# A fused attention and mixer kernel on one core: engines in program order, 1 KB load runs, a wide index load, gated weights

## The chip, the cores and the metric

The kernel runs on one core of one Trainium2 chip. The metric is the device time of one execution in microseconds. The kernel before takes 393.94 us (median of three runs, 393.15 to 394.01). "Span" is the length of the one execution that was profiled; it is some 0.3 to 4 us shorter than the median time. Positions such as "at 87.4 us" are counted from the start of the span.

## The reference

Eight batches go through a windowed attention with eight global tokens and then through a token-and-channel mixer. Cut to what matters:

```python
# q, k, v: (8 batches, 8 heads, 576, 64) f32; global_idx: 8 sorted positions, int64
scores = q @ k.T / 8, kept where |i - j| <= 32 or i or j is global
x = softmax(scores) @ v                       # heads side by side: (8, 576, 512)
u = x + (relu(x.T @ w_tok1) @ w_tok2).T       # w_tok1 576x256, w_tok2 256x576
out = u + relu(u @ w_ch1) @ w_ch2             # w_ch1 512x1536, w_ch2 1536x512
```

## The kernel before

Per batch the work falls into a "sparse" and a "dense" part. The sparse part is attention and token mixer: transposes `T` of q and k (tile `pT`), scores `S_` (tile `s`), keys and outputs of the global tokens `GK` and `OG` (tiles `gk`, `og`), P.V (tile `pv`), then the token matmuls `M1` (tile `a1p`) and `M2` (tile `hp`), whose result plus x is u. `M3` transposes u into uT. The dense part is the channel mixer: `M4` (tile `b1p`, 12 pieces) reads uT, `M5` (tile `op`) writes the output. The function `merge` weaves the sparse part of batch b+1 into the dense part of batch b. Batch 0 has no dense part to hide behind: everything before its first `b1p` is the start.

The parts that the argument touches:

```python
# index list: 8 of 16 int32 words per partition, so 1,024 pieces of 4 bytes in all
nc.scalar.dma_start(out=gidx_b, in_=bass.AP(tensor=gt32, offset=0, ap=[[0, P], [2, NG]]))
# [...] q and k of batch 0 head by head in 256-byte runs, then v, on the sync queue

def globals_(b):                       # global keys into q's tile: needed by the first scores
    nc.gpsimd.tensor_copy(out=qTs[b % 2][:, :, :, 0:NG], in_=gT[:, b]...)

def PV(b, tau):
    ps = psv([P, 2, 512], name=f"pv_{b}_{tau}")        # the only buffer of its kind
    # [...] 18 matmuls, then reciprocal and multiply on VectorE

def M3(b, part):                       # u -> uT by DMA, for every batch
    nc.sync.dma_start_transpose(out=s["uT"][:, :, ...], in_=s["u16"][:, tau, :])

# start; the tile scheduler may move instructions
for p in range(NP):
    cast0(p); T(0, p)
    if p == 0: gather_t(0); globals_(0)
    S_(0, p)
for c in range(NT): castv0(c)          # v: f32 -> f16 on GpSimd
GK(0); OG(0)
# load_wc1, load_wc2, load(1), gather(1), five PV, M1, M2, M3 of batch 0 [...]
gather_t(1)
for b in range(B):
    # [...]
    merge(sparse(b + 1) if b + 1 < B else [], dense(b))
```

The softmax here doesn't subtract the row's maximum and nothing guards it: scores larger than these inputs give would overflow.

## Time and profile before

| stage of the kernel before | from, us | to, us | what limits it |
|---|---|---|---|
| to the first scores | 0 | 44.6 | loads, then a copy on GpSimd |
| first scores to first `og` | 44.6 | 58.6 | scores, exponentials, masks |
| `og` to the first `b1p` | 58.6 | 87.35 | P.V, token matmuls, transposing of u |
| two batches, for instance | 166.6 | 244.7 | TensorE, 78.2 us for a pair |
| last dense part and store | 361.0 | 391.9 | TensorE, then the store |

The busy table of the page, kernel before. Its columns are engine, busy us, share of the span, instructions:

```profile
span 391.9 us, 6622 instructions
...
PE 319.8 (82%) x2697; PEld 167.3 (43%) x2697; DVE 185.6 (47%) x400; ACT 137.2 (35%) x269; POOL 114.7 (29%) x156
```

TensorE (PE) is busy for 82% on average. The average hides two very different stages, as the busy table in stretches shows. Its columns: stretch, its length, the busy time of each engine with its instruction count, the granted TensorE clock, the mean DMA share and GB/s:

```profile
0.00:30.00 30.00, 2.14 (x17) 1.65 (x17) 13.83 (x70) 2.80 (x6) 12.49 (x28) 1.00 0.69 113
...
58.60:87.35 28.75, 17.21 (x149) 9.61 (x149) 12.69 (x27) 2.49 (x4) 20.81 (x26) 0.82 1.58 114
...
166.56:244.72 78.16, 76.71 (x675) 39.97 (x673) 42.19 (x80) 32.89 (x65) 25.83 (x32) 1.00 0.88 92
```

In the loop TensorE works 76.7 of 78.2 us. In the first 30 us it works 2.1, and in the 29 us before the loop 17.2. The clock column is an upper bound there: this profile has no clock record before 67.4 us, and the view counts what is missing as 1.00.

The waits of TensorE in the first 90 us, kernel before (who waited for whom; us in total, times, longest):

```profile
PE pT_0_266 L347 <- ACT qn_79 L328: 23.1, 1, 23.1
PE s_0_0_288 L364 <- POOL qT_168 L339: 14.5, 1, 14.5
PE pT_0_266 L347 <- DVE kn_81 L328: 4.8, 1, 4.8
```

The first line is the wait for q to land and be cast. The DMA view of the stretch from 4 to 12 us says why it is so long:

```profile
DMA packets 807, 0.00 MB, mean 0 GB/s; under 512 B 807, under 2 KB 807, under 8 KB 807
## 3 DMA queue, kind: packets, MB, share of 16 engines
q10 hardware_dynamic: 807, 0.00, 4.4%
```

For 8 us nothing moved but the 4-byte pieces of the index list (queue q10). The q and k loads had been issued on another queue and moved nothing: that queue stood for 8.9 us (3.9 to 12.8 us). The pieces went at 101 a us, so about 0.16 us a piece if 16 engines shared them evenly (an estimate from the 101), though the engines were busy with them for only 4.4% of the time. The second wait, 14.5 us, is the first score matmul behind the copy of the global keys, which GpSimd does only after a cast of v.

The waits of TensorE from 90 to 345 us, kernel before, the longest three:

```profile
PE b1p_0_3083 L509 <- DMA uT_3004<-u_5_2972: 1.3, 1, 1.3
PE b1p_0_1117 L509 <- DMA uT_1038<-u_1_1006: 0.8, 1, 0.8
PE b1p_0_2100 L509 <- DMA uT_2021<-u_3_1989: 0.7, 1, 0.7
```

Only these three batch ends of the stretch wait for the transposed u.

### The profile page before, as it was taken

The page shows a single profiled execution, that of the slowest core. Times are in us where ns is not written, and L with a number is a line of the kernel's source. Part 1 is how long each engine was busy: PE and PEld are TensorE (multiplying, and loading weights), DVE is VectorE, ACT ScalarE, POOL GpSimd, SP SyncE. Part 2 cuts the span into 40 slices and gives each one's busy share as a digit, 9 for nine tenths or more (in the row PEclk, how much of TensorE's full clock was granted, in tenths as well). Part 3 has the DMA queues.
Part 4 walks back from the last instruction along what each step waited for, and adds up shares of the span by engine and source line. Part 5 has one row for each costly group of instructions (what it writes and reads, how often), then busy time and mean ns, then how long its engine had stood idle before and what let it go on. Part 6 is the DMA issues. An engine that isn't in the chain of part 4 may idle for free.

```text
span 391.9 us, 6622 instructions
## 1 busy us (share of the span) xinstructions
PE 319.8 (82%) x2697; PEld 167.3 (43%) x2697; DVE 185.6 (47%) x400; ACT 137.2 (35%) x269; POOL 114.7 (29%) x156
## 2 busy tenths in 40 slices
PE   0010255659999999999999999999899999997995
PEld 0010234324454465444544654455446545453552
DVE  5342254344645563566445635664456356644012
ACT  2001250106710861077118610761086107710610
POOL 4520798922820372028203720282000000000000
PEclk9999999688999999999999999999999999999999
DMA  0799999991985398419853984298600041005012
GB/s 14 122 198 206 182 141 94 122 114 8 125 79 147 21 115 75 136 30 129 79 147 22 117 75 135 35 126 81 145 0 2 28 136 28 2 28 149 0 55 80
DMA packets 143071, 34.56 MB, mean 88 GB/s; under 512 B 134336, under 2 KB 138304, under 8 KB 143040
## 3 DMA queue, kind: packets, MB, share of 16 engines
q0 software_dynamic: 102832, 16.42, 56.1%
q1 hardware_dynamic: 33776, 8.26, 11.2%
q10 hardware_dynamic: 6432, 9.44, 7.2%
q8 instruction: 21, 0.34, 0.4%
q14 instruction: 10, 0.08, 0.1%
HBM read 36.11 MB, written 9.44 MB: 116 GB/s over the span
## 4 chain that ended last, share of the span: by engine, by line
PE 59%; ACT 9%; DMA 3%; DVE 1%; SPq 1%; issue 1%; ACTq 0%
ACT e_all L374 2%; ACT e_all L383 2%; ACT e_all L382 1%; ACT e_all L381 1%; SPq L498 1%; DMA out_dram<-osb_0_2979 1%; DMA uT_3972<-u_7_3940 1%; PE op_4_4213 L535 1%; PE op_2_3013 L535 1%; PE op_2_2030 L535 1%; PE op_2_1047 L535 1%; PE op_2_3981 L535 1%; PE op_0_2938 L535 1%; PE op_0_3463 L535 1%; PE op_3_4197 L535 1%
## 5 line engine op out<-in xcount | busy, mean ns | idle before, releaser
L509 PEld LDWEIGHTS <-wc_184 128*128 128x128 f16 x384 | 33.0, 98 | 45.1 <-issue 15.8
L390 DVE TENSOR_TENSOR e_all<-e_all,bandm 128x1040 f16<-128x1040 f16 x64 | 42.4, 704 | 0.5
L123 POOL DMA_DIRECT2D qn_80<-in_q_dram x20 | 17.5, 873 | 60.6 <-PE pT_3_1738 L347 22.8
L439 PEld LDWEIGHTS <-e_all 128*128 128x128 f16 x320 | 25.2, 101 | 2.1 <-issue 1.0
L123 POOL DMA_DIRECT2D qn_79<-in_q_dram x15 | 13.2, 883 | 40.2 <-PE pT_3_1217 L347 20.1
L384 DVE TENSOR_TENSOR eg<-e_all,bandm 128x160 f16<-128x160 f16 x32 | 7.7, 242 | 31.0 <-ACT e_all L383 31.0
L128 POOL DMA_DIRECT2D vsh_84<-in_v_dram x20 | 16.9, 865 | 14.4 <-PE pv_2_916 L444 1.5
L347 PE MATMUL pT_0_266<-ident,qn_79 128*128 128x128 f16 x5 | 0.7, 309 | 23.1 <-ACT qn_79 L328 23.1
L444 PEld LDWEIGHTS <-e_all 128*128 128x128 f16 x256 | 19.0, 101 | 1.3
L347 PEld LDWEIGHTS <-qn_79 128*128 128x128 f16 x80 | 6.1, 106 | 28.4 <-ACT qn_79 L328 23.1
L364 PEld LDWEIGHTS <-kT_170 64*128 64x128 f16 x160 | 6.2, 103 | 27.4 <-issue 13.8
L123 POOL DMA_DIRECT2D kn_82<-in_k_dram x20 | 17.6, 878 | 0.0
L128 POOL DMA_DIRECT2D vsh_83<-in_v_dram x15 | 12.7, 881 | 9.6 <-PE b1lp_0_1385 L522 1.1
L328 ACT CAST qn_79<-n_q 64x128 f16<-64x128 f32 (+1 forms) x8 | 3.4, 456 | 32.8 <-DMA n_q<-in_q_dram 32.8
L481 PEld LDWEIGHTS <-w_183 128*128 128x128 f16 x80 | 8.2, 103 | 12.6 <-issue 4.8
L123 POOL DMA_DIRECT2D kn_81<-in_k_dram x15 | 13.3, 888 | 0.0
L364 PE MATMUL s_0_0_288<-qT_168,kT_170 64*128 64x208 f16 x4 | 0.5, 357 | 14.5 <-POOL qT_168 L339 14.5
L336 POOL CAST vsh_83<-n_v 32x512 f16<-32x512 f32 (+1 forms) x9 | 6.2, 697 | 19.3 <-DMA n_v<-in_v_dram 19.1
L522 PEld LDWEIGHTS <-wc_184 128*128 128x128 f16 x192 | 11.1, 98 | 0.6
L364 PEld LDWEIGHTS <-kT_171 64*128 64x128 f16 x160 | 5.2, 95 | 12.8 <-issue 8.5
L463 PEld LDWEIGHTS <-w_181 128*128 128x128 f16 x64 | 6.3, 101 | 6.4 <-issue 1.9
L539 DVE TENSOR_TENSOR osb_0_4162<-u_7_3940,op_0_4149 128x512 f32<-128x512 f16 x1 | 0.7, 689 | 17.1 <-PE op_0_4149 L535 17.1
(1059 smaller groups left out, 821.1 us busy)
## 6 DMA issues: line engine op xcount, KB each, us to landing
qn_80<-in_q_dram POOLq DMA_DIRECT2D x16, 128.0 KB, 4.6
kn_82<-in_k_dram POOLq DMA_DIRECT2D x16, 128.0 KB, 4.6
wc_184<-in_moe_w_ch_dram POOLq DMA_DIRECT2D x3, 512.0 KB, 10.3
wc_185<-in_moe_w_ch_dram POOLq DMA_DIRECT2D x3, 512.0 KB, 8.0
vsh_84<-in_v_dram POOLq DMA_DIRECT2D x12, 128.0 KB, 3.5
qn_79<-in_q_dram POOLq DMA_DIRECT2D x12, 128.0 KB, 4.2
kn_81<-in_k_dram POOLq DMA_DIRECT2D x12, 128.0 KB, 4.2
n_q<-in_q_dram SPq DMA_DIRECT2D x9, 128.0 KB, 7.6
```

Of the source, the lines that this page charges most:

```text
L123: nc.gpsimd.dma_start(out=dst[b % 2][0:n, t], in_=ten[b, :, P * t : P * t + n, :].rearrange("h p d -> p h d"))
L128: nc.gpsimd.dma_start(out=vsh[b % 2][r0:r1, c, :, 0:D], in_=v[b, :, j0 : j0 + (r1 - r0), :].rearrange("h p d -> p h d"),)
L364: nc.tensor.matmul(ps[:, par, off : off + n], lhsT=kT[r, P * c : P * c + P], rhs=qf[r, lo : lo + n], start=True, stop=True,)
L374: nc.scalar.activation(out=e2[:, :, 1:3, 64:EW], in_=s1[:, :, 0 : 2 * W].rearrange("p h (c x) -> p h c x", c=2), func=AF.Exp, scale=scale)
L383: nc.scalar.activation(out=e2[:, :, 3, 64:EW], in_=s2[:, :, 2 * QS : 2 * QS + W], func=AF.Exp, scale=scale)
L390: nc.vector.tensor_mul(out=eh, in0=eh, in1=bandm)
L439: nc.tensor.matmul(o, lhsT=e_all[:, h, tau, EW - P - sh : EW - sh], rhs=vsh[b % 2][:, tau, h, :], start=False, stop=last and tau == NT - 1,)
L444: nc.tensor.matmul(o, lhsT=e_all[:, h, tau + 1, 0:P], rhs=vsh[b % 2][:, tau + 1, h, :], start=False, stop=last)
L481: nc.tensor.matmul(ps[:, i, :], lhsT=w2[:, ch, P * tau - sh : P * tau - sh + P], rhs=s["a1"][:, ch, :], start=(ch == 0), stop=(ch == 1),)
L509: nc.tensor.matmul(ps, lhsT=wc1[:, cc, P * j : P * j + P], rhs=s["uT"][:, cc, :], start=(cc == 0), stop=(cc == 3))
L522: nc.tensor.matmul(ps[:, i, :], lhsT=wc1[:, cc, P * j : P * j + P], rhs=s["uTl"][:, cc, :], start=(cc == 0), stop=(cc == 3),)
L535: nc.tensor.matmul(ps, lhsT=w, rhs=wc2[:, j, :], start=(j == 0), stop=(j == NJ - 1))
```

## The change

Its intent: start the dense work earlier and spend less time on changes of TensorE's tile shape. All engines now run in program order, and the weave of the loop groups matmuls of one shape. The first two batches of q and k come in runs of four rows (1 KB) and are put in order when they leave PSUM. The index list comes as one 64-byte row per partition. The channel weights are issued only behind casts. Besides, and not in the headline: the global keys are copied on VectorE, P.V has two half-size buffers, batch 1 is loaded like batch 0 on the sync queue, the output stores moved from ScalarE's queue to the sync queue, zeroing moved from VectorE to GpSimd, and batch 0's u is transposed on TensorE.

The core of the diff (cuts marked):

```diff
-    psV = ctx.enter_context(tc.tile_pool(name="psV", bufs=1, ...PSUM))
+    psV = ctx.enter_context(tc.tile_pool(name="psV", bufs=2, ...PSUM))
+    ctx.enter_context(tc.manual_schedule())
-    gidx_b = const.tile([P, NG], I32)
+    gidx_b = const.tile([P, NG, 2], I32)
-    nc.scalar.dma_start(out=gidx_b, in_=bass.AP(... ap=[[0, P], [2, NG]]))
+    nc.scalar.dma_start(out=gidx_b.rearrange("p g w -> p (g w)"), in_=bass.AP(... ap=[[0, P], [1, 2 * NG]]))
+    def load_qk(b, hs):      # 1 KB runs: partition p holds rows 4p .. 4p+3
+        for ten, dst in ((q, lq), (k, lk)):
+            nc.sync.dma_start(out=dst[:, hs].rearrange("p h i d -> p h (i d)"),
+                in_=ten[b, hs, 0 : S - LAST, :].rearrange("h (p i) d -> p h (i d)", i=4))
-    nc.vector.memset(e_all[:, :, :, 0:64], 0.0)     # and the other zeroing
+    nc.gpsimd.memset(e_all[:, :, :, 0:64], 0.0)
     def globals_(b):
-        nc.gpsimd.tensor_copy(
+        nc.vector.tensor_copy(
     # [...] PV: two tiles [P, 512] instead of one [P, 2, 512]
     def M3(b, part):
+        if part < 2 and b == 0:
+            pu = psv([P, 2, 4, P], F16, name=f"pu_{b}_{part}")   # 8 transposes on TensorE, one copy
     def sparse(b):           # (weight, piece); merge places by weight
-        u += [(0.6, lambda p=p: T(b, p)) for p in range(2)]
-        # [...]
-        u += [(3.0, lambda: None)]
+        u = [(8.0 if b == 1 else 0.5, lambda: globals_(b))]
+        u += [t(0), t(1), sa(0), sb(0), t(2), sm(0), ...]        # t(p): weight 1.0
+        # [...]
+        u += [(6.0, lambda: (M2(b, 2), M3(b, 2) if b % 2 else None))]
     # [...] start: castv(0), then load_wc1; after batch 1's casts of q and k, load_wc2; then castv(1)
```

## The prediction

> **What bounds the kernel now.** Three stretches, by the busy table in stretches and TensorE's timeline. (1) The start: the first dense matmul (b1p of batch 0) begins at 87.4 us; TensorE is under 60% busy until 70 us. (2) From 87.4 to 361 us the dense part of batch b is mixed with the attention of batch b+1; TensorE is 97-99% busy, 78.2 us for two batches. (3) The last dense part and store, 31 us.
>
> **The start.** Two things hold the first q and k tiles. The index load (1,024 four-byte packets on its queue, landing 14.4 us after its issue): the DMA packets show about 106 of these a microsecond from 3 to 13 us, and no q or k packet between 4 and 12 us. Then the weights share the engines until 34 us (q and k get 40 KB/us, against 215-245 alone). The first scores wait for the global keys, copied on GpSimd behind the cast of v (the wait of 14.5 us); they start at 44.6 us and take 3.85 us per head pair.
>
> After the change the index is one 64-byte packet per partition, q and k are 1 KB packets, wc1 is issued after the casts of v, wc2 after batch 1's casts, and the global keys are copied on VectorE. First head pair at 6-8 us, all of q and k by 13 us. VectorE in program order is then the limit: per head pair a cast 0.6, four copies about 1.5, three mask products 1.6 us, and once 8 us of masks and gather: done near 34 us. P.V with the first token matmul takes about 10 us, then relu, two adds of 1.2 us and the transposes on TensorE: first dense matmul at about 53 us, a gain near 34 us. All of it is on the critical path.
>
> **Steady state.** A change of tile shape costs 0.09-0.10 us: a matmul before a score starts the next 0.315 us later, against 0.216. [...] The order shows 123 changes against 143: 2 us. Two P.V buffers and ordered ScalarE work may remove 3 us of short waits.
>
> Against that stands the end of each batch. From the end of the first token-output matmuls (hp) to uT ready takes 7.8 us: one add of 1.22, four transposes of 1.24 issued one after the other, 2.4 landing. In the new order TensorE has 5.2 us of work there when b is odd, 6.5 when even, and the next batch's first transposes now stand behind b1p_0. So TensorE should wait about 2.5 us at each odd and 1.3 at each even boundary, against 0.8-1.3 at odd ones alone before: some 9 us lost.
>
> Sum: 394 - 34 - 2 - 3 + 9 = 364 us. Range 354 to 377.
>
> **What would show it right.** First b1p_0 near 53 us (48-59); no gap in q/k packets between 4 and 12 us; the 78 us pair becomes 79-82 us; waits of TensorE at b1p_0 for the DMA of uT, about 2.5 and 1.3 us.
>
> **What would make it wrong.** The start may be set by v, wc1 or the gather instead of VectorE (first dense matmul past 60 us); wc2, issued late, may hold the first M5; or the transposes may be ready sooner than I count, which gives 9 us more gain.
>
> Chances: faster by over 2% 0.95, within 2% 0.04, slower 0.01.

## The result and the profile after

The changed kernel takes 376.04 us (median of four runs, 375.0 to 377.74), against 393.98 us for the kernel before in the same rounds. The ratio is 0.9549, with a 95% interval of 0.9503 to 0.9596. Ratios here and below are the mean time of one kernel's fast runs over that of the other's fast runs of the same rounds, so not quite the ratio of the medians. The experiments ran in different rounds, in which the median of the kernel before itself lay between 393.98 and 395.35 us. So a difference between the medians of two experiments is uncertain by some 1.4 us.

The busy table of the page and the stretches, kernel after:

```profile
span 375.8 us, 6776 instructions
...
PE 319.2 (85%) x2713; PEld 168.2 (45%) x2713; DVE 202.4 (54%) x507; ACT 136.6 (36%) x269; POOL 117.3 (31%) x167
```

```profile
0.00:20.80 20.80, 3.71 (x27) 2.55 (x28) 12.64 (x44) 2.92 (x5) 17.86 (x41) 1.00 0.93 204
...
36.60:58.45 21.85, 14.79 (x138) 8.72 (x139) 13.03 (x33) 1.59 (x3) 15.58 (x19) 0.92 1.02 210
...
144.12:225.63 81.51, 76.99 (x672) 40.34 (x673) 44.48 (x109) 32.71 (x65) 25.14 (x30) 0.98 0.85 89
```

The first scores now begin at 20.8 us, the first `og` at 36.6, the first `b1p` at 58.45. But a pair of batches takes 81.5 us instead of 78.2, with the same TensorE work. Set against the kernel before on the two spans: the start gave 28.9 us, the first mixed batch (dense part of batch 0) cost 4.8, the rest of the loop 7.8; together 16.3 gained, the spans differ by 16.1.

The waits of TensorE in the first 90 us, kernel after:

```profile
PE pT_0_215 L370 <- ACT qn_83 L352: 8.7, 1, 8.7
PE pg_260 L325 <- DVE g_q_168 L324: 3.2, 1, 3.2
PE pcol_238 L283 <- DVE isgb L279: 3.2, 1, 3.2
PE pT_2_314 L370 <- DVE kn_85 L352: 2.5, 1, 2.5
PE pg_260 L325 <- DVE g_k_170 L324: 2.0, 1, 2.0
```

The two long waits are gone; four of these five are now waits for VectorE. The DMA view from 4 to 12 us, kernel after, answers the one of before:

```profile
DMA packets 2769, 2.15 MB, mean 268 GB/s; under 512 B 859, under 2 KB 2734, under 8 KB 2769
...
q1 hardware_dynamic: 2576, 2.07, 90.1%
...
q10 hardware_dynamic: 124, 0.01, 0.8%
```

Where nothing landed before, 2 MB now land, q and k above all. The waits of TensorE from 90 to 345 us, kernel after:

```profile
PE b1p_0_2209 L571 <- DMA uT_2150<-u_3_2136: 2.8, 1, 2.8
PE b1p_0_3240 L571 <- DMA uT_3181<-u_5_3167: 2.7, 1, 2.7
PE b1p_0_1178 L571 <- DMA uT_1111<-u_1_1104: 2.6, 1, 2.6
PE b1p_0_4240 L571 <- DMA uT_4197<-u_7_4183: 2.5, 1, 2.5
PE b1p_0_2760 L571 <- DMA uT_2695<-u_4_2678: 1.4, 1, 1.4
PE b1p_0_3776 L571 <- DMA uT_3726<-u_6_3709: 1.3, 1, 1.3
```

Now every batch end of the loop waits for uT: 2.5 to 2.8 us where the batch is odd, 1.3 to 1.4 where it is even. (The even end of batch 2 is put down to VectorE by the same view, with 1.2 us.) The seven together are 14.5 us, 9.8 more than before. The stretches on either side of the first of these ends, kernel after, show something else:

```profile
97.30:100.70 3.40, 0.36 (x2) 0.29 (x3) 1.55 (x7) 0.00 (x0) 0.00 (x0) 1.00 0.68 132
100.70:104.10 3.40, 3.11 (x15) 1.78 (x15) 0.14 (x1) 0.60 (x1) 0.00 (x0) 0.50 0.30 97
```

TensorE's granted clock is 0.50 for a record of 3.41 us that begins at 100.7 us, right after the wait. It costs about 1.7 us, half of the record's length. There are three such records in the loop after, behind the ends of batches 1, 3 and 5, and none in the loop before once its first `b1p` are over (one record ends at 91.3 us).

### The profile page after: what moved, and what is told of

It is laid out like the page before. It is cut to its first block, busy times and chain, and to the rows that moved or that the text cites. A ratio compares the mean times of both kernels' runs of the same rounds, so it can differ in the third digit from the quotient of the medians.

```text
span 375.8 us, 6776 instructions
## 1 busy us (share of the span) xinstructions
PE 319.2 (85%) x2713; PEld 168.2 (45%) x2713; DVE 202.4 (54%) x507; ACT 136.6 (36%) x269; POOL 117.3 (31%) x167
## 4 chain that ended last, share of the span: by engine, by line
PE 71%; DVE 12%; ACT 6%; DMA 6%; SPq 3%; issue 2%; DVEq 0%; ACTq 0%
SPq L560 3%; DMA lq<-in_q_dram 1%; DVE e_all L434 1%; ACT e_all L415 1%; ACT e_all L424 1%; DMA uT_1111<-u_1_1104 1%; ACT e_all L422 1%; ACT e_all L423 1%; PE op_4_4431 L597 1%; PE op_3_3737 L597 1%; PE op_4_1695 L597 1%; PE op_3_2706 L597 1%; PE op_3_4415 L597 1%; PE op_2_4399 L597 1%; PE op_1_4383 L597 1%
## 5 line engine op out<-in xcount | busy, mean ns | idle before, releaser
L571 PEld LDWEIGHTS <-wc_180 128*128 128x128 f16 x384 | 32.8, 99 | 55.1 <-issue 22.4
L340 POOL DMA_DIRECT2D qn_83<-in_q_dram x15 | 13.5, 898 | 46.1 <-PE pT_3_1297 L370 23.4
L340 POOL DMA_DIRECT2D qn_84<-in_q_dram x15 | 13.2, 879 | 40.8 <-PE pT_3_2873 L370 20.1
L345 POOL DMA_DIRECT2D vsh_87<-in_v_dram x15 | 12.8, 895 | 16.6 <-PE pv_1_1_1516 L489 2.5
L345 POOL DMA_DIRECT2D vsh_88<-in_v_dram x15 | 12.6, 839 | 16.0 <-PE pv_1_1_982 L489 1.5
L340 POOL DMA_DIRECT2D kn_85<-in_k_dram x15 | 13.6, 907 | 0.0
L532 PEld LDWEIGHTS <-w_179 128*128 128x128 f16 x80 | 7.9, 100 | 12.2 <-issue 4.3
L340 POOL DMA_DIRECT2D kn_86<-in_k_dram x15 | 13.3, 888 | 0.0
L370 PEld LDWEIGHTS <-qn_83 128*128 128x128 f16 x80 | 7.1, 119 | 13.6 <-ACT qn_83 L352 9.2
L584 PEld LDWEIGHTS <-wc_180 128*128 128x128 f16 x192 | 10.9, 98 | 0.6
L370 PEld LDWEIGHTS <-kn_85 128*128 128x128 f16 x80 | 6.8, 120 | 4.8 <-DVE kn_85 L352 4.4
L512 PEld LDWEIGHTS <-w_177 128*128 128x128 f16 x64 | 5.6, 99 | 5.0
L370 PEld LDWEIGHTS <-qn_84 128*128 128x128 f16 x80 | 5.7, 98 | 3.5
L597 PEld LDWEIGHTS <-b_7_4239 128*128 128x128 f16 x48 | 4.7, 98 | 5.4
```

The source lines that it names most:

```text
L340: nc.gpsimd.dma_start(out=dst[b % 2][0:n, t], in_=ten[b, :, P * t : P * t + n, :].rearrange("h p d -> p h d"))
L345: nc.gpsimd.dma_start(out=vsh[b % 2][r0:r1, c, :, 0:D], in_=v[b, :, j0 : j0 + (r1 - r0), :].rearrange("h p d -> p h d"),)
L370: nc.tensor.transpose(out=pT[:, ti, P * t : P * t + P], in_=n[b % 2][:, t, 2 * p : 2 * p + 2, :], identity=ident)
L532: nc.tensor.matmul(ps[:, i, :], lhsT=w2[:, ch, P * tau - sh : P * tau - sh + P], rhs=s["a1"][:, ch, :], start=(ch == 0), stop=(ch == 1),)
L571: nc.tensor.matmul(ps, lhsT=wc1[:, cc, P * j : P * j + P], rhs=s["uT"][:, cc, :], start=(cc == 0), stop=(cc == 3))
L584: nc.tensor.matmul(ps[:, i, :], lhsT=wc1[:, cc, P * j : P * j + P], rhs=s["uTl"][:, cc, :], start=(cc == 0), stop=(cc == 3),)
```

## The experiments

There are two questions. What made the start shorter, and what took back a large part of it? For the first, the theory was that the index row and the copy of the global keys do it; the rivals were the 1 KB runs, the gated weights, and the program order. For the second, the theory was that the batch ends are at fault, because the next batch's transposes moved behind the first `b1p`; the rival was that the transposed u is late whatever stands before it.

### One: the next batch's transposes ahead of the first `b1p`

```diff
-        return (1.0, lambda: (T(b, p), TE(b, p)))
+        return (0.0 if b > 1 and p < 2 else 1.0, lambda: (T(b, p), TE(b, p)))
-    u = [(8.0 if b == 1 else 0.5, lambda: globals_(b))]
+    u = [(8.0 if b == 1 else 0.0, lambda: globals_(b))]
```

> The kernel after, with the next batch's first two groups of transposes (and its first two score matmuls) put ahead of b1p_0, as the kernel before had them. Theory 1 (the loop loses at the end of each batch, where TensorE waits for the transposed u): the waits at b1p_0, 3.0 us at odd and 1.5 at even boundaries, fall below 0.5 us, the half-clock record of 3.4 us that follows each odd boundary goes, the odd batches pay about 1.2 us for a relu that is now uncovered; about 363 us. Rival (the loop is slower because VectorE and ScalarE have more work in it): the two batches stay at 81 us and the total at 375-376.

Measured: 365.49 us (363.49 to 366.99), ratio 0.9256 (0.922 to 0.9291). The waits of TensorE from 90 to 345 us in this run, and TensorE in order of time at the end of batch 3:

```profile
PE s L404 <- DVE kT L393: 3.5, 6, 0.7
PE hp L532 <- ACT a L516: 3.5, 3, 1.2
PE b1p L571 <- DMA uT<-u: 1.2, 1, 1.2
```

```profile
174.51 0.44 PE L370 MATMUL pT<-ident,kn 128*128 128x128 f16 x5
175.52 0.35 PE L404 MATMUL s<-qT,kT 64*128 64x208 f16 x4 [0.57 <-DVE kT L393]
175.81 1.04 PE L571 MATMUL b1p<-uT,wc 128*128 128x512 f16 x4
```

The first `b1p` now follows the scores without a wait, a pair of batches takes 77.8 us, and there is no record of half clock in the loop. Two edited lines gave back 10.5 us of the medians (376.04 to 365.49); by the ratios it is 11.5. The theory is confirmed. The view also shows what is left: 0.6 to 0.7 us at six ends before the first scores, whose q and k have just been transposed, and up to 1.2 us at the relu between `a1p` and `hp`. The 1.2 us at `b1p` are the end of batch 7, which has no next batch whose transposes could go ahead.

### Two: the token matmuls earlier instead

```diff
-        u += [(6.0, lambda: (M2(b, 2), M3(b, 2) if b % 2 else None))]
+        u += [(10.0, lambda: (M2(b, 2), M3(b, 2) if b % 2 else None))]
```

> The kernel after, with the last weight of the attention list 10 instead of 6, so that the token matmuls come earlier and more dense matmuls stand between hp and the next b1p_0 (7.8 us at odd, 9.1 at even boundaries). Theory 1: the same as for the transposes put ahead: waits under 0.5 us, no half clock, about 363 us. Rival (VectorE and ScalarE work): 375-376, or slower, since the attention is squeezed into fewer dense matmuls.

Measured: 369.66 us (367.57 to 369.94), ratio 0.9331 (0.9291 to 0.9371). A larger last weight leaves more dense work behind the token matmuls. The 363 us that I expected were missed. It covers the even ends wholly and leaves 1.3 and 1.5 us at the ends of batches 3 and 5. New waits come from the narrower weave: 0.7 us between scores and 0.8 us before `pv`, three times each, and 1.2 us at the relu, four times. So it is the work between u and its reader that matters, and the transposes are the cheaper way to put it there. No record of half clock falls on these shorter waits.

### Three: the zeroing of e_all away from GpSimd

In the start, one cast of VectorE lasts as long as GpSimd's memset beside it. VectorE, kernel after, in order of time:

```profile
17.13 2.33 DVE L324 CAST g_k_170<-g_k_166 128x128 f16<-128x128 f32 x1
```

GpSimd at the same moment, kernel after:

```profile
17.12 2.26 POOL L254 MEMSET e_all<- 128x2560 f16 x1
19.33 0.60 POOL L255 MEMSET e_all<- 128x512 f16 x1
```

The same cast takes 0.21 us in the kernel before. Here it begins just as the memset does and ends with it (2.33 us beside 2.26). Why they would hold each other up, no run here shows. The run below tests whether the memset is what stretches the cast.

```diff
-    nc.gpsimd.memset(e_all[:, :, :, 0:64], 0.0)      # and two more
+    for h in range(H):
+        zero_(e_all[:, h, :, 0:64])                  # nc.scalar.copy from a zero tile, after cast0(1)
```

> The kernel after, with the three memsets of e_all in the start taken from GpSimd to ScalarE, which is idle then. Theory 2 [...]: the cast of g_k takes 0.2 us instead of 2.33, and the first b1p_0 comes 2 to 3 us earlier, total 373-374. Rival (the cast only looks long, and the gathered keys or the DMA were late): b1p_0 stays at 58.4 us.

Measured: 374.01 us (373.38 to 375.57), ratio 0.9466 (0.9426 to 0.9505). VectorE in this run:

```profile
17.11 0.65 DVE L330 CAST g_k<-g_k 128x128 f16<-128x128 f32 x1
```

The first `b1p` begins at 54.65 us instead of 58.45. Only part of these 3.8 us is the zeroing's. The first `og` begins at 34.59 us instead of 36.56, 2.0 us earlier, and the time is 2.0 us shorter. The other 1.8 us lie behind `og`: a half-clock record fell at 52.9 us in the start of the kernel after and not in this one. Experiment one has the start of the kernel after unchanged, also without that record, and its first `b1p` begins at 55.94 us. So the zeroing is worth 1.3 to 2.0 us. This run also sizes that record: batch 3, with a record behind its odd end, takes 43.40 us from first `b1p` to first `b1p`; batch 5, without, takes 41.67. The difference is 1.7.

### Four: the index row alone, in the kernel before

```diff
-    nc.scalar.dma_start(out=gidx_b, ... ap=[[0, P], [2, NG]]))
+    nc.scalar.dma_start(out=gidx_b.rearrange("p g w -> p (g w)"), ... ap=[[0, P], [1, 2 * NG]]))
```

> The kernel before, with the index loaded as one row of 64 bytes per partition and nothing else changed. Theory 3 (the four-byte packets hold every other load for about 9 us): q and k packets flow from 3 us on, the first scores come near 36 instead of 44.6 us, total about 385. Rival (the start is bound by bytes that share the queues and by v, not by the index): less than 3 us of gain.

Measured: 387.13 us (386.24 to 388.56), ratio 0.9792 (0.9751 to 0.9833). The first `b1p` begins at 80.58 instead of 87.35 us and the loop is unchanged. The longest waits of TensorE in the first 90 us of this run:

```profile
PE s L364 <- POOL qT L339: 18.1, 1, 18.1
PE pT L347 <- ACT qn L328: 13.1, 1, 13.1
```

q arrives 10 us sooner (13.1 instead of 23.1), but the scores then wait 18.1 instead of 14.5 us for the global keys behind v. So 6.8 us of the start are the index row's.

### Five: the 4-byte index load back, in the kernel after

```diff
-    gidx_b = const.tile([P, NG, 2], I32)
+    gidx_b = const.tile([P, NG], I32)          # and its load and its reader
```

> The kernel after, with the index loaded again in four-byte pieces. Theory 3: the loads stand still from about 4 to 12 us again and the first b1p_0 comes 8 to 9 us later, total about 384. Rival (the 1 KB runs and the gated weights already hide it): under 3 us of loss.

Measured: 381.76 us (381.04 to 382.84), ratio 0.9667 (0.963 to 0.9703). The first `b1p` moves from 58.45 to 64.57 us. The queue of q and k stands still again, from 3.9 to 12.4 us. From both sides the index row is worth 6 to 7 us.

### Six: weights not gated; seven: no 1 KB runs

```diff
# six
     load_wt()
+    for h0 in range(0, NJ, 4): load_wc1(h0)
+    for h0 in range(0, NJ, 4): load_wc2(h0)     # and not behind the casts
# seven
-                in_=ten[b, hs, 0 : S - LAST, :].rearrange("h (p i) d -> p h (i d)", i=4),
+                in_=ten[b, h, 0 : S - LAST, :].rearrange("(t p) d -> p t d", p=P),   # one DMA per head, plain copies
```

How two queues share the engines can be read from the kernel before. From 20 to 24 us the queue of q and k moved 611 packets of 256 bytes and GpSimd's queue 609 of 1 KB, about one for one, and q and k got 39 KB a us; alone, from 35 to 40 us, they got 224.

> The kernel after, with wc1 and wc2 issued right after the token weights instead of after the casts. Theory 4: q and k have landed by then, but v shares the engines packet by packet and lands near 35-40 us instead of 20, so OG and P.V come 5 to 8 us later: total about 382. Rival (gating matters little once the index is a row): within 2 us of 376. Rival (gating is the main part of the gain): over 10 us later.

> The kernel after, with q and k of the first two batches in runs of 256 bytes (one DMA per head) and the plain copies after the transposes. Theory: the load is slower (about 225 against 330 KB per us), the first head pair lands about 1 us later and all of q and k near 14 us, but VectorE, which sets the pace there, has 0.45 us less to copy per head pair: within 2 us of 376 either way. Rival (the 1 KB runs are a main part of the gain): 3 us or more slower.

Measured: without the gate 375.58 us (374.52 to 377.01), ratio 0.951 (0.9471 to 0.955); without the long runs 376.86 us (375.98 to 377.19), ratio 0.9537 (0.9504 to 0.957). Both equal the kernel after. Of the first I had expected 382 us, and missed. v's last piece was cast at 31.6 us instead of 24.3, but `og` began at 35.0 us and VectorE's last mask product of batch 0 ended at 38.2, so v was not what ended last. The edit moved something else too: GpSimd's zeroing came at 21.4 to 25 us, away from the cast of the gathered rows that it stretched in the kernel after (0.20 us here, see three). `og` began 1.5 us earlier and the first `b1p` at 55.8 us. So the equal times may hide a loss of some 1.5 to 2 us by the missing gate. Of the second: 1 KB packets moved at 295 to 348 KB a us and 256-byte packets at 179 to 225, and the last k landed at 17.9 us instead of 14.1. But VectorE's first cast began at 8.72 us instead of 8.73, and the plain copies out of PSUM were shorter: 0.42 instead of 0.69 us. The first `b1p` even came 2.1 us earlier, at 56.38 us, and the loop gave that back. Each of the two was undone alone. Each may stand in for the other: with 1 KB runs q and k are in at 14.1 us (kernel after) and ungated channel weights are issued at 14.57 us (experiment six); with the gate the 256-byte runs are in at 17.9 us, and the engines move nothing from 24 to 26 us before the channel weights come (experiment seven). Undoing both together was not run.

### Eight: the scheduler's order back

```diff
-    ctx.enter_context(tc.manual_schedule())
```

> The kernel after, with the scheduler's own order instead of program order. Theory: the loop keeps the same order within a few instructions, so its 81 us per two batches stay; the start may change: total 372-382. Rival (program order is a main part of the gain): 384 or more.

Measured: 371.19 us (369.34 to 372.69), ratio 0.9395 (0.9346 to 0.9444). The same source without the fixed order is 4.9 us faster, so program order is no source of the gain. That is just under the range that I expected. The first `b1p` came at 57.47 us. The first mixed batch took 39.1 us instead of 42.5; the batch ends waited as after.

### Nine: index row and global keys on VectorE, in the kernel before

```diff
# besides the index row
     def globals_(b):
-        nc.gpsimd.tensor_copy(
+        nc.vector.tensor_copy(
```

> The kernel before with the index as one row and the global keys copied on VectorE instead of behind v's cast on GpSimd. Theory (the second large part of the gain is that the first scores no longer stand behind v): first scores near 22 us instead of 37.8; then the output of the global keys waits for v's cast, which ends near 44 us as in the run with the row alone; first dense matmul near 73 us instead of 80.6; time near 380 us against 387 with the row alone. Rival (the wait for the global keys was hidden behind v and behind P.V): scores early, but the first dense matmul still past 79 us and the time 386 to 388 us.

Measured: 388.04 us (385.66 to 389.34), ratio 0.9805 (0.9747 to 0.9862): nothing over the row alone. The first scores began at 21.3 us, and `og` at 44.5, 7.3 us before the run with the row alone. I expected that number, but v was not what set it: its cast ended at 42.1 us. The scores of the second head pair came only at 34.05 us, because the cast of its q waited for the load. ScalarE in this run:

```profile
29.27 0.62 ACT L328 CAST qn<-n_q 128x512 f16<-128x512 f32 x1 [11.28 <-DMA n_q<-in_q_dram]
```

Weights were on the DMA engines in the same time, from 12 to 32 us; four loads of channel weights are issued at 14.00 to 17.64 us. In the kernel after, with gate and 1 KB runs, that cast comes at 9.49 us. So the two together, each worth nothing when undone alone, may well be worth several us; that is not shown by a run. After `og`, P.V stood. VectorE in order of time in this run:

```profile
51.42 0.69 DVE L451 TENSOR_TENSOR x<-pv,rr 128x512 f16<-128x512 f32 x1
57.83 0.23 DVE L311 CAST g_q<-g_q 128x128 f16<-128x128 f32 x1 [5.72 <-DMA g_q<-in_q_dram,idx_i]
60.32 0.52 DVE L311 CAST g_k<-g_k 128x128 f16<-128x128 f32 x1 [2.26 <-DMA g_k<-in_k_dram,idx_i]
60.46 0.38 DVE L450 RECIPROCAL rr<-pv 128x8 f32<-128x8 f32 x1
```

In VectorE's order two casts of rows gathered for batches 4 to 7 stand between two steps of P.V. GpSimd issues that gather behind the 15 loads of batch 1, from 54 us on, so the rows land at 58 and 60 us. P.V has one buffer and waits 7.5 us. My theory of the second large part had the right first half; the win was eaten by the next thing in line.

### Ten: and the second gather's transposing moved

```diff
-    gather_t(1)            # before the loop
     for b in range(B):
+        if b == 1:
+            gather_t(1)
```

> The kernel before with the index as one row, the global keys copied on VectorE, and the transposing of the second gather moved from the start into batch 1. Theory (in the run before this one the 7.3 us that the earlier scores won were eaten by P.V, which stood 7.5 us behind a cast of rows gathered for later batches, in VectorE's order): no wait of P.V over 2 us, first dense matmul at 69 to 72 us against 78.2, time near 380 us (378 to 382) against 388. Rival (the scheduler's order or the transposing DMA gives the wait back at another place): first dense matmul past 75 us, time 385 to 388.

Measured: 387.44 us (385.93 to 389.86), ratio 0.9844 (0.9795 to 0.9892). The first `b1p` came at 79.40 us. A miss, but not a test of what it was meant for. VectorE in this run:

```profile
51.87 0.69 DVE L451 TENSOR_TENSOR x<-pv,rr 128x512 f16<-128x512 f32 x1
57.41 0.23 DVE L311 CAST g_q<-g_q 128x128 f16<-128x128 f32 x1 [4.84 <-DMA g_q<-in_q_dram,idx_i]
```

I moved the lines in the source, and the scheduler put the casts back at the same place between the same two steps. An edit has to be checked in the built order, not in the source. How the remaining 22 us of the start's gain divide among the copy of the global keys, the loads of the later head pairs (gate and 1 KB runs together), batch 1's load on the sync queue, the second gather, the two P.V buffers and the transposes of u on TensorE is left open. What can be read off is where they lie:

| kernel | first scores | first `og` | first `b1p` | `og` to `b1p` |
|---|---|---|---|---|
| before | 44.6 | 58.6 | 87.35 | 28.8 |
| index row | 37.7 | 51.8 | 80.58 | 28.8 |
| index row, keys on VectorE | 21.3 | 44.5 | 78.16 | 33.7 |
| after | 20.8 | 36.6 | 58.45 | 21.9 |
| the best version below | 18.1 | 27.0 | 47.29 | 20.3 |

### Eleven and twelve: versions that beat both

The first takes experiment one and fixes what it left: one more dense piece between `a1p` and `hp` at odd ends, and the next batch's first transposes one dense piece earlier.

```diff
-        u += [(2.0, lambda: PV(b, 4)), (1.8, ...M1...)]
+        u += [(2.0, lambda: PV(b, 4)), (3.0 if b % 2 else 1.8, ...M1...)]
-        u += [(6.0, lambda: (M2(b, 2), M3(b, 2) if b % 2 else None))]
+        u += [(3.6, lambda: (M2(b, 2), M3(b, 2) if b % 2 else None))]     # 10.0 for the last batch
+        u += [(5.6 if b == 1 else 4.4 if b % 2 else 3.2, lambda: (T(b + 1, 0), TE(b + 1, 0)))]
```

The second has besides, in the start:

```diff
-    nc.gpsimd.memset(e_all[...])               # and pads, weight tails
+    nc.vector.memset(e_all[...])               # while VectorE waits for k
-    cast_qk(0, ..., (nc.scalar.copy, nc.vector.tensor_copy))
+    cast_qk(0, ..., (nc.scalar.copy, nc.scalar.copy))
+    # masks before the first tile; T of three head pairs before the gathered rows;
+    # M2(0, 1) ahead of M3(0, 0); 256-byte runs for batch 0; GpSimd's pads after the weights' issue;
+    # wc2 issued right behind wc1; batch 1's q cast and one copy of the transposed u on ScalarE
```

> The kernel after with the repaired batch ends (the next batch's transposes ahead of the first dense matmul) and, besides, one dense piece between the first token matmul and the second while ScalarE does the relu at odd ends, and the next batch's first transposes one dense piece earlier. Theory (the repaired kernel's remaining waits of 1.33 us at the relu, four times, and 0.74 us before the first scores, six times, are worth their length): pair of batches near 75.5 us instead of 77.8, time near 357 us (353 to 361) against 365.5. Rival (waits only move, since the attention part is squeezed into less dense work): 363 to 367 us.

> The same, and besides in the start: zeroing of e_all, pads and weight tails on VectorE before the first cast instead of on GpSimd beside VectorE's casts, k's casts on ScalarE, masks before the first tile, transposes of all head pairs before the gathered rows are needed, two token-output products ahead of the transposes. Theory (VectorE's work, stretched by GpSimd, sets the start): first dense matmul at 43 to 47 us instead of 55.9, time near 346 us (342 to 352). Rival (the arrival of v, of wc1 or of the gathered rows sets it): first dense matmul past 51 us, time 352 to 358 us.

That GpSimd stretches VectorE's work is what experiment three measured for one cast: 2.33 us beside the memset, 0.65 without.

Measured: 363.21 us (361.05 to 364.04), ratio 0.9184 (0.913 to 0.9237), and 360.03 us (359.53 to 361.73), ratio 0.9122 (0.9078 to 0.9166). Both beat both kernels; both miss what I expected.

The first came out in the rival's range. From batch 2's first `b1p` to batch 3's it took 35.50 us instead of 36.96, from batch 6's to batch 7's 35.21 instead of 36.21. But between them, from batch 4's to batch 5's, it took 37.41 instead of 36.95, with a wait of 1.8 us for uT, and the other stretches did not change at all: 40.86 against 40.82 us from batch 3's to batch 4's. The wait before the scores was taken away there and no time came of it; what took its place I did not find.

In the second, the start did as the theory said, within 0.3 us of its range: the first `b1p` at 47.29 us. Of the 9.0 us gained over the first version 6.0 were lost in the first mixed batch, 48.6 instead of 42.65 us. TensorE's waits from 47 to 100 us in that run:

```profile
PE b1p L587 <- DMA uT<-u: 5.4, 1, 5.4
PE s L413 <- ACT e_all L424: 3.3, 2, 2.3
```

The DMA packets show loads of later batches on the engines until about 94 us in this run, beside the transposing DMA of batch 1's u, whose pieces took 6.7 us (median) from issue to landing; in experiment one those loads are over by 89 us and the pieces took 2.6. That the one delays the other is argued from this and not shown by a run. A half-clock record of 6.83 us from 92.2 us on lies in this stretch too and takes its part: the three matmuls of `b1p` from 95.92 us on took 1.44 us, where four took 1.04 in experiment one.

## Why the prediction was right or wrong

**Right: the direction, the range, and what the start waited on.** Both long waits of the start were read rightly: the 4-byte index load (6 to 7 us, from both sides) and the copy behind v (the scores began at 21.3 us once it was on VectorE). The first pair of q and k landed at 8.0 and 8.7 us, the last at 12.9 and 14.1. What the copy was worth in time is not shown: in experiment nine it gave nothing over the row alone. So "all of it is on the critical path" stays unproven for that part.

**Right: the batch ends.** The prediction counted 7.8 us from the end of `hp` to uT and 5.2 or 6.5 us of work for TensorE in it, and so waits of 2.5 and 1.3 us and some 9 us lost. Measured: 2.5 to 2.8 and 1.2 to 1.4 us, 9.8 more than before in all. (It overlooked that batch 7's end waited 2.0 us before.) Experiment one shows the cause.

**Right: the price of a tile-shape change.** A change costs 0.093 to 0.097 us each way in both kernels, as the trace before had it: a matmul of 512 columns starts the next one of another shape 0.309 to 0.312 us later, against 0.216; the way back takes 0.182 and 0.205 us after matmuls of 208 and 256 columns, whose columns account for 0.088 and 0.108 (worked out from the 0.216 for 512). Why, no run here shows. The 20 changes fewer that it counted are then some 1.9 us of 394 (an estimate: 20 times 0.095), not the point of the change.

**Wrong: "First dense matmul at about 53 us, a gain near 34 us."** It began at 58.45, a gain of 28.9. The step that failed is VectorE's sum in the start. Its last mask product of batch 0 ended at 39.0 us, not "near 34". The terms per head pair held or nearly so (casts 0.6 to 1.1 us, copies 1.5, mask products 1.6). The mis-sized term is "once 8 us of masks and gather": it took 13.0 us (masks 8.9 and gather 4.0, from their records in the trace). Part of that is the zeroing, which the change moved to GpSimd, into the same microseconds: the cast of the gathered keys became 2.33 us instead of 0.21. The diff showed that move and I priced it as free. Products that build the masks were stretched too, beside GpSimd's cast of v, which the zeroing does not explain; two of them took 0.63 and 0.70 us in experiment three too. VectorE and GpSimd, kernel after:

```profile
22.58 0.63 DVE L302 SCALAR_TENSOR_TENSOR bandm<-band,rowok,colng 128x64 f16<-128x64 f16 x1
```

```profile
20.46 3.85 POOL L359 CAST vsh_87<-lv 32x512 f16<-32x512 f32 x6
```

The smallest of these products take 0.28 and 0.34 us in the kernel before and 0.63 and 0.70 here. That GpSimd is the cause of this second part is argued from the times alone. Experiment three got 2.0 us back at `og`. In the best version, where VectorE zeroes by itself while it waits for k, the same masks and gather took 8.7 us, and the first `b1p` came at 47.29. From VectorE's end to the first `b1p` the prediction counted 19 us and 19.5 passed, but that is luck: experiment one, with the same start and without the half-clock record at 52.9 us, took 17.0. I put the 2.5 us between them down to the clock: half of that record's 3.41 us is 1.7 of it; that the rest is a later rise to full speed is my estimate and shown by no figure here.

**Missing: the granted clock.** The sum had no term for it. Three waits at odd ends were each followed by a record at half clock, 1.7 us each, 5.1 in all (an estimate: three times the 1.7 that experiment three shows). Those waits were 2.6 to 2.8 us long; the end of batch 7 waited 2.5 us, and no such record followed.

The traces show how busy TensorE was before such a record. In the kernels before and after the lengths of the clock records are multiples of 3.41 us (3.41, 6.83, 10.24 and so on; each run's last record left out). I cut fourteen traces into stretches of that length on the grid of the records. In the 32 stretches at full clock that half clock followed, TensorE's busy share was 0.49 or less, and 0.11 to 0.29 at the three ends of the kernel after. In the 1,238 stretches at full clock that it did not follow, the lowest share was 0.40. Between 0.40 and 0.49 both happened. In the kernels before and after alone it is 6 stretches with shares of 0.11 to 0.41, and 175 others with 0.43 or more. The wait of batch 7 lay across two stretches, with shares of 0.73 and 0.53.

**Mis-sized: the rest of the loop.** "2 us" and "3 us of short waits" should have saved 5; the loop without ends and clock records saved 2.5 (12.6 lost, where the ends and the clock account for 10 and 5.1). In the first mixed batch program order cost rather than saved: it was 3.4 us shorter without it in experiment eight.

The sum: on the spans the prediction was 13.7 us too hopeful (30 against 16.3). The start is 5.1 of it (VectorE 5.0 late, the clock of the start 2.5 as put above, the rest 2.4 better than counted), the loop's clock 5.1, the batch ends 1.0, the rest of the loop 2.5. The measured 376.04 us lies 1 us inside the upper end of the range.

## What to carry to other kernels

Count, at every hand-over between stages, how much other work stands between the last producer and the first reader; moving two pieces across that line was worth more here (10.5 us) than the whole grouping by tile shape. A short wait of TensorE can cost clock besides: behind a wait of 2.6 us it was 1.7 us more here, behind the waits of 1.3 us, and behind one of 2.5, nothing. When zeroing moves to GpSimd, look at what VectorE does in the same microseconds (here a cast of 0.21 us took 2.33 beside a memset of 2.26); and when a wait is taken away and nothing is won, look for the next wait in the same engine's order before giving up the theory.
